# A quarter of w3 on the hardware DMA queue, q first on the software queue, and a new order of the pieces, in an attention + maxout-FFN kernel

## Chip, cores and metric

One Trainium2 chip, one of its cores. The metric is the device time of one execution in microseconds (us), as the median of several runs. PE is TensorE (matmuls and, as PEld, its weight loads), DVE is VectorE, ACT is ScalarE, POOL is GpSimd, SP is SyncE, which here only issues DMAs.

## What is computed

```
# q, k, v: (8, 8, 576, 64), phi: (8, 8, 576, 32), fp32; w1, w2, w3: (512, 768), w_out: (768, 512)
a = softmax(phi, axis=2)                       # over the sequence, per memory slot
k_m = einsum('bhsm,bhsd->bhmd', a, k)          # 32 memory rows per head
v_m = einsum('bhsm,bhsd->bhmd', a, v)
attn = softmax(q @ k_m^T / sqrt(64), axis=-1)  # over the 32 slots
x = (attn @ v_m), heads side by side           # 4608 rows of 512
h = maximum(maximum(x @ w1, x @ w2), x @ w3)
out = h @ w_out                                # (4608, 512) fp32
```

## The kernel before

The eight batches are worked on one by one, in bf16 with fp32 sums in PSUM. Four pairs of heads lie side by side, with 128 partitions each. The kernel never forms x. It multiplies v_m into the weights first (`fold`), so that the FFN's first layer runs on the attention weights. It also uses max(x w1, x w2, x w3) = max(x (w1 - w3), x (w2 - w3), 0) + x w3: the relu and the max are done on the differences, and x w3 w_out is a term of its own, for which w3 @ w_out is formed once (`w3_t` transposes w3, `w3_o` multiplies).

The program is a long list of pieces, written out by hand, each as letter, index and batch: `F3@1` is piece F3 of batch 1. The list (lines 593 to 619) is the program order on every engine. Each engine works through its own instructions in this order and waits where an input isn't there. A second list (line 138) gives the PSUM bank of each piece that uses one. The pieces:

- loads: `H` k and v of batch 0 in halves (H2, H0 are k; H3, H1 are v), `L0` phi, `L1` k, `L2` v, `L3` q, `Y0`, `Y1`, `Y2` w1, w2, w3, `Y3` w_out. All but phi of batch 0 are issued by POOL (the software queue) and cast from fp32 to bf16 on the way. phi of batch 0 goes over SP's hardware queue in fp32. Loads of POOL land in the order of their issue.
- `E` exp of phi (ACT). `r0`, `r1` pack k and v into `kvr` (`pack`, POOL). `B` multiplies a with k and v (`att_kv`, PE; from batch 2 on it reads `kvr`, and so both packs). `N` normalises (DVE). `K` transposes (PE and a copy).
- `Q` transposes q (DVE). `S` is the scores and their exp (PE, then ACT twice).
- the softmax over the slots, for each of two groups of heads: `a` transpose, `s` sum, `c` reciprocal (DVE), `m` multiply (`att_mul`, POOL), `X` transpose back (DVE). Batch 0 uses `M` and `R` (matmul with ones, logarithm and exp) in place of `a`, `s`, `c`, `m`.
- `D` folds v_m into the weights (PE and a copy). `V` forms w1 - w3 and w2 - w3 (DVE); batch 0 does without by a second term in `D`.
- `F` is the FFN's first layer: twelve pieces per batch, even ones with a relu copy, odd ones with a max on DVE. `T` is the second layer and the output's DMA. `W`, `O` are w3_t and w3_o. `Z` are matmuls on zeros (fillers) that keep PE busy while data are on their way, and `I` is the identity matrix.

`evacuate` (line 166) does the copies out of PSUM: a table `EVAC` names ACT or DVE for each piece, and a `!` behind the piece in the list swaps the two. `issue` (line 561) hands the `!` to the pieces K, D, F, T, W and O. The other kinds of piece don't take it.

```
"m": lambda: att_mul(b, i),                # no swap: POOL
"D": lambda: fold(b, i, swap),
```

Of the kernel before, what the change touches and what calls it, by code (L numbers as in the profile page):

```python
# [8 lines left out]
FP32 = mybir.dt.float32  # L9
# [6 lines left out]
def kernel(  # L16
# [12 lines left out]
    nc = tc.nc  # L29

    B, H, S, D = q.shape
    M = phi.shape[-1]
    P = 128
    NP = H // 2
    NG = NP // 2
    HP = P // 2
    NC = S // HP
    R = 32
    DM = H * D
    DF = moe_w1.shape[1]  # L40
# [5 lines left out]
    inp = ctx.enter_context(tc.tile_pool(name="inp", bufs=2))  # L46
# [23 lines left out]
    w_sb = const.tile([P, NP, 3, DF], BF16, name="w_sb")  # L70
# [7 lines left out]
    def by_pair(src, b):  # L78
        return src[b].rearrange("h s d -> (h s) d").rearrange(
            "(j p c) d -> p j (c d)", p=P, c=NC  # L80
        )
# [1 line left out]
    halves = [slice(0, NP // 2), slice(NP // 2, NP)]  # L83

    def load_ph(b):
        ph = inp.tile([P, NP, NC, M], FP32, name="ph")
        loaded.setdefault(b, {})["ph"] = ph
        dst = ph.rearrange("p j c m -> p j (c m)")
        if b == 0:
            for h in halves:  # L90
                nc.sync.dma_start(out=dst[:, h], in_=by_pair(phi, b)[:, h])
        else:
            nc.gpsimd.dma_start(out=dst, in_=by_pair(phi, b))

    def load_kv(b, i, h=slice(0, NP)):
        kv = loaded.setdefault(b, {})["kv"] = kvos[b % 2]
        nc.gpsimd.dma_start(  # L97
            out=kv[:, 1 - i, h].rearrange("p j c d -> p j (c d)"),
            in_=by_pair((k, v)[i], b)[:, h],
        )  # L100

    def pack(b, i):
        nc.gpsimd.tensor_copy(  # L103
            out=kvrs[b % 2][:, :, :, D * i : D * (i + 1)], in_=kvos[b % 2][:, 1 - i]
        )

    def load_q(b):
        qq = inp.tile([P, NP, NC, D], BF16, name="qq")
        loaded.setdefault(b, {})["q"] = qq
        nc.gpsimd.dma_start(  # L110
            out=qq.rearrange("p j c d -> p j (c d)"), in_=by_pair(q, b)
        )

    def load_w(i):
        w = (moe_w1, moe_w2, moe_w3)[i]
        nc.gpsimd.dma_start(
            out=w_sb[:, :, i], in_=w.rearrange("(j p) f -> p j f", p=P)
        )

    ident = const.tile([P, P], BF16, name="ident")  # L120
# [1 line left out]
    def load_wo():  # L122
        nc.gpsimd.dma_start(out=wo_sb, in_=moe_w_out.rearrange("(t p) c -> p t c", p=P))

    load_ph(0)

    warm = const.tile([P, BANK], BF16, name="warm")
    nc.vector.memset(warm, 0.0)  # L128
# [4 lines left out]
    for i in range(P // M):  # L133
# [4 lines left out]
    banks = iter(  # L138
        "".join(
            """  # L140
            00224460026701101401264026402640264026452063420643064206420642064562074206742064
            20642064201640264102640264026402640264072406247026402640264024602406520462046204
            62704267402640264124602416420642064206420642067676767670
            """.split()
        )
    )
# [78 lines left out]
    def att_exp(b, js=slice(0, NP)):  # L225
        s = st.setdefault(b, {})
        if "e" not in s:
            s["e"] = work.tile([P, NP, NC, M], BF16, name="e")
        nc.scalar.activation(out=s["e"][:, js], in_=loaded[b]["ph"][:, js], func=AF.Exp)  # L229
# [8 lines left out]
    def att_kv(b, part=None):  # L238
        s = st[b]
        kvp = two_banks()  # L240
        s["kvp", part] = kvp
        kv = loaded[b]["kv"]
        nd = {None: 2 * D + 1, 0: 2 * D, 1: D}[part]
        kvr = kvrs[b % 2]
        for c in range(NC):
            for j in range(NP):
                for a in range(NG):
                    r = slice(HP * a, HP * (a + 1))
                    nc.tensor.matmul(  # L249
                        kvp[M * j : M * (j + 1), a, 0:nd],  # L250
                        lhsT=s["e"][r, j, c, :],
                        rhs={
                            None: lambda: kvr[r, j, c, 0:nd],
                            0: lambda: k_and_ones(kv, r, j, c),
                            1: lambda: kv[r, 0, j, c, :],
                        }[part](),
                        start=(c == 0),
                        stop=(c == NC - 1),
                        tile_position=(HP * a, M * j),
                    )  # L260
# [141 lines left out]
    def att_rec(b, g):  # L402
        s = st[b]
        nc.vector.reciprocal(out=s["sm", g], in_=s["sm", g])  # L404
# [156 lines left out]
    def issue(b, n, swap):  # L561

        i = int(n[1:]) if len(n) > 1 else None
        {
            "I": lambda: [make_identity(nc, ident)]
            + [nc.gpsimd.memset(x[:, :, :, 2 * D : 2 * D + 1], 1.0) for x in kvrs],
            "Y": lambda: load_w(i) if i < 3 else load_wo(),
            "L": lambda: load_ph(b) if i == 0 else load_q(b) if i == 3 else load_kv(b, i - 1),
            "H": lambda: load_kv(b, i % 2, halves[i // 2]),
            "r": lambda: pack(b, i),  # L570
            "E": lambda: [att_exp(b, h) for h in (halves if b == 0 else [slice(0, NP)])],
            "B": lambda: att_kv(b, i),
            "N": lambda: att_kv_norm(b, i),
            "K": lambda: att_kv_t(b, swap, i),
            "Q": lambda: att_q(b, i),
            "S": lambda: att_score(b),
            "a": lambda: att_t(b, i),
            "s": lambda: att_sum(b, i),
            "c": lambda: att_rec(b, i),
            "m": lambda: att_mul(b, i),  # L580
            "X": lambda: (ones_mul if (b, i) in ONES else att_back)(b, i),
            "M": lambda: ones_sum(b, i),
            "R": lambda: ones_rec(b, i),
            "D": lambda: fold(b, i, swap),
            "F": lambda: ffn1(b, i, swap),
            "T": lambda: ffn2(b, i, swap),
            "W": lambda: w3_t(i, swap),
            "O": lambda: w3_o(i, swap),
            "V": lambda: w_diff(i),
            "Z": lambda: warm_up(i),  # L590
        }[n[0]]()


    for w in """
        E@0 H2@0 H0@0 L3@0 Z25@0 B0@0 Y2@0 I@0 N0@0 Z2@0 K0@0! Q0@0 Q1@0 Z9@0 S@0 Z2@0 M0@0 M1@0
        R0@0 R1@0 W0@0 Y3@0 W1@0 W2@0 Z6@0 O1@0 H3@0 O3@0 O2@0 H1@0 X1@0 B1@0 X0@0 N1@0
        K1@0 O0@0 Y0@0 D1@0! D0@0! D3@0 F8@0 F10@0 F2@0 V0@0 F6@0 F0@0! Y1@0 D2@0 D4@0 F4@0
        L0@1 V1@0 F1@0 E@1 F3@0 L1@1 F5@0 F9@0 F7@0 L3@1 F11@0 B0@1 T3@0 N0@1 K0@1! L2@1 Q1@1
        L2@2 L1@2 Q0@1 L0@2 V2@0 T0@0! L3@2 S@1 T1@0 a0@1 s0@1 c0@1 m0@1 B1@1 N1@1 a1@1 L1@3
        K1@1 s1@1 D0@1 D1@1! D2@1 c1@1 m1@1 X0@1 L3@3 r1@2 X1@1 T2@0! L2@3 F6@1 F10@1 F7@1 F2@1  # L600
        F3@1 F4@1 F0@1 r0@2 E@2 F5@1 F1@1 F11@1 L0@3 L0@4 F8@1 L2@4 F9@1 B@2 D3@1 N@2 Q1@2
        T0@1! K@2 T2@1! r0@3 Q0@2 S@2 a0@2 a1@2 s1@2 c1@2 m1@2 T4@1! D1@2! s0@2 D2@2 c0@2 m0@2
        X1@2 D0@2 T3@1 Q0@3 L3@4 X0@2 Q1@3 T1@1 F0@2 F4@2 F8@2 F6@2 F9@2 E@3 F7@2 r1@3 F5@2
        F10@2 F1@2 B@3 L1@4 D3@2 N@3 L0@5 F2@2 F11@2 E@4 F3@2 L1@5 K@3 r1@4 L2@5 T2@2! S@3 T3@2
        a0@3 s0@3 c0@3 m0@3 D0@3 D2@3 a1@3 s1@3 c1@3 X0@3 D1@3! Q0@4 m1@3 T1@2 L3@5 L2@6 T0@2!
        X1@3 F10@3 r0@4 F2@3 F4@3 E@5 Q1@4 r0@5 F5@3 F3@3 L1@6 F8@3 B@4 N@4 D3@3 F9@3 F6@3
        F11@3 L0@6 K@4 F0@3 F7@3 F1@3 S@4 a0@4 T4@3! s0@4 a1@4 D0@4 c0@4 s1@4 r1@5 c1@4 D3@4
        m0@4 X0@4 Q0@5 T0@3! D1@4! D2@4 B@5 T3@3 m1@4 X1@4 L0@7 F10@4 Q1@5 N@5 F8@4 K@5 F6@4
        F9@4 S@5 F7@4 L3@6 F2@4 F4@4 a0@5 L1@7 a1@5 F0@4 s0@5 r1@6 F3@4 D0@5 r0@6 s1@5 c1@5 E@6
        D3@5 m1@5 c0@5 F1@4 T1@3 L2@7 F11@4 L3@7 E@7 F5@4 m0@5 B@6 D1@5! D2@5 X1@5 N@6 T2@3!  # L610
        X0@5 F6@5 F8@5 Q0@6 Q1@6 K@6 F4@5 F9@5 S@6 F7@5 r0@7 a0@6 F2@5 a1@6 s0@6 c0@6 F0@5
        F10@5 m0@6 F1@5 s1@6 c1@6 F11@5 F5@5 T0@4! F3@5 X0@6 T2@4! r1@7 D0@6 D1@6! Q0@7 B@7
        m1@6 N@7 X1@6 T2@5! K@7 T3@4 Q1@7 S@7 a0@7 F2@6 s0@7 a1@7 s1@7 c1@7 m1@7 c0@7 F4@6
        T4@5! D3@6 D2@7 D0@7! T0@5! D3@7 D2@6 X1@7 m0@7 D1@7! T1@4 X0@7 F6@7 F3@6 T1@5 F4@7
        F8@7 F0@7 F5@6 F10@6 F7@7 F9@7 F10@7 F5@7 F0@6 F11@7 F6@6 F1@7 F7@6 F2@7 F8@6 F11@6
        F9@6 F1@6 F3@7 T0@6! T0@7! T3@5 T2@7! T2@6! T1@6 T1@7 T3@6 T4@7! T3@7
    """.split():
        n, b = w.rstrip("!").split("@")
        issue(int(b), n, w.endswith("!"))
# [30 lines left out]
```

## Time and profile before

| what | value |
|---|---|
| median of 3 runs | 164.98 us (164.94 to 165.61) |
| span of the profiled execution | 163.3 us |
| granted TensorE clock, mean | 0.995 |
| bytes by the software queue (POOL) | 21.43 MB, 68.7% of 16 engines' span |
| bytes by SP's hardware queue | 9.90 MB, 17.2% |
| longest group on PE | F, line 466: 384 matmuls, 50.5 us |
| longest group on POOL | packs, line 103: 12 of 2.11 us |
| multiplies on POOL, line 409 | 14 of 1.15 us |

The profile is of one execution. Its span is counted from the first to the last instruction. The times of the runs are those of whole executions, and are somewhat longer. "L103" is line 103 of the kernel. The matmuls of PE overlap, so a group's mean is longer than what one adds to the time.

### The profile page before, as it was taken

The numbers are of one execution on the slowest core, as the hardware profiler recorded it, in microseconds if no ns is written. First come the engines' busy times: TensorE is split into PE (matmuls) and PEld (weight loads), VectorE is DVE, ScalarE is ACT, GpSimd is POOL, SyncE is SP. The second block draws the span as 40 slices with busy tenths as digits, with TensorE's granted clock in tenths as the row PEclk, the third lists the DMA queues.
The fourth block names the chain that finished last, engine by engine and source line by source line (L and its number), as shares of the span: only waits on it lengthen the run. The fifth ranks groups of instructions, "written<-read, shape, count | busy, mean of one in ns | idle before, by whom it ended". The sixth has DMA issues, their size and how long they took to land.

```text
span 163.3 us, 4838 instructions
## 1 busy us (share of the span) xinstructions
PE 153.8 (94%) x2080; PEld 85.3 (52%) x2080; DVE 90.4 (55%) x181; ACT 100.6 (62%) x151; POOL 69.5 (43%) x71
## 2 busy tenths in 40 slices
PE   7978798899899999999999999999999999999990
PEld 2433444564377436743673575576553468744450
DVE  2023704798838665849399748879749128810010
ACT  4205445845497488778885899994658976223320
POOL 7932205100599259657968957646403100000000
PEclk9999999999999999999999999999999999999998
DMA  6999999999999999999999999996313130014333
GB/s 150 152 206 207 205 210 217 274 208 210 253 313 238 209 253 379 274 210 293 252 263 206 232 355 264 191 233 150 130 69 129 69 128 0 0 68 186 135 128 130
DMA packets 21974, 31.77 MB, mean 195 GB/s; under 512 B 1216, under 2 KB 16576, under 8 KB 21952
## 3 DMA queue, kind: packets, MB, share of 16 engines
q0 software_dynamic: 16080, 21.43, 68.7%
q1 hardware_dynamic: 5728, 9.90, 17.2%
q8 instruction: 16, 0.26, 0.6%
q10 hardware_dynamic: 144, 0.13, 0.2%
q14 instruction: 6, 0.05, 0.1%
HBM read 39.32 MB, written 9.44 MB: 299 GB/s over the span
## 4 chain that ended last, share of the span: by engine, by line
PE 83%; DMA 9%; POOL 2%; ACT 2%; issue 1%; DVE 1%; ACTq 0%; POOLq 0%
PE psum L497 29%; PE psum L466 28%; DMA wo_sb<-in_moe_w_out_dram 9%; PE psum L506 8%; PE psum L440 6%; PE psum L249 4%; PE psum L192 3%; PE psum L333 2%; PE psum L515 1%; ACT h L170 1%; PE psum L538 1%; PE psum L298 1%; POOL kvo L97 1%; ACT wp L172 1%; POOL qq L110 0%
## 5 line engine op out<-in xcount | busy, mean ns | idle before, releaser
L497 PE MATMUL psum<-wo_sb,hT 128*128 128x512 bf16 x210 | 51.3, 380 | 0.0
L466 PE MATMUL psum<-attn,wp 128*128 128x288 bf16 x384 | 50.5, 286 | 0.1
L479 DVE TENSOR_TENSOR hT<-psum,h 128x576 bf16<-128x576 f32 x48 | 34.2, 749 | 18.0 <-PE psum L466 12.5
L466 PEld LDWEIGHTS <-wp 128*128 128x128 bf16 x384 | 36.7, 98 | 13.2 <-issue 2.0
L172 ACT COPY ot<-psum 128x512 f32<-128x512 f32 x35 | 20.7, 591 | 32.1 <-PE psum L506 25.2
L497 PEld LDWEIGHTS <-hT 128*128 128x128 bf16 x210 | 19.2, 97 | 24.0 <-issue 4.3
L172 ACT CAST wp<-psum 128x1024 bf16<-128x1024 f32 (+1 forms) x31 | 29.2, 995 | 3.8 <-PE psum L440 2.0
L103 POOL COPY kvr<-kvo 128x2304 bf16<-128x2304 bf16 x12 | 25.3, 2111 | 13.7 <-DMA kvo<-in_k_dram 10.1
L170 ACT ACTIVATE h<-psum 128x576 bf16<-128x576 f32 x47 | 28.4, 659 | 3.5 <-PE psum L466 3.3
L409 POOL TENSOR_TENSOR t<-t,sm 128x576 bf16<-128x576 bf16 x14 | 16.1, 1154 | 24.6 <-DVE sm L404 24.4
L506 PE MATMUL psum<-wp,attn 128*128 128x512 bf16 x62 | 18.4, 379 | 0.0
L159 PE MATMUL psum<-warm 128*128 128x512 bf16 x44 | 12.1, 427 | 1.2 <-DVE warm L128 1.2
L313 DVE STREAM_TRANSPOSE qT<-qq 128x576 f32<-128x576 f32 x16 | 11.7, 747 | 1.4 <-DMA qq<-in_q_dram 1.4
L342 ACT ACTIVATE e<-psum 128x576 bf16<-128x576 f32 x16 | 9.6, 652 | 3.8 <-PE psum L333 3.8
L229 ACT ACTIVATE e<-ph 128x1152 bf16<-128x1152 f32 (+1 forms) x9 | 9.6, 1065 | 1.7 <-DMA ph<-in_phi_dram 1.6
L395 DVE TENSOR_REDUCE sm<-t 128x18 f32<-128x576 bf16 x14 | 10.3, 738 | 0.2
L387 DVE STREAM_TRANSPOSE t<-e 128x288 f32<-128x288 f32 x14 | 6.4, 465 | 6.2 <-ACT e L342 6.1
L97 POOL DMA_DIRECT2D kvo<-in_v_dram x9 | 6.7, 749 | 7.1 <-PE psum L249 4.1
L506 PEld LDWEIGHTS <-attn 128*128 128x128 bf16 x62 | 6.1, 98 | 7.1
L110 POOL DMA_DIRECT2D qq<-in_q_dram x8 | 6.2, 770 | 6.6 <-DVE h L174 3.7
L555 DVE COPY ot<-psum 128x256 f32<-128x256 f32 x1 | 0.4, 425 | 15.4 <-PE psum L546 15.4
L249 PEld LDWEIGHTS <-e 64*32 64x32 bf16 x720 | 6.9, 90 | 3.7 <-issue 3.3
(57 smaller groups left out, 114.4 us busy)
## 6 DMA issues: line engine op xcount, KB each, us to landing
out_dram<-ot SPq DMA_DIRECT2D x35, 256.0 KB, 5.6
qq<-in_q_dram POOLq DMA_DIRECT2D x8, 576.0 KB, 12.2
ph<-in_phi_dram POOLq DMA_DIRECT2D x7, 576.0 KB, 14.4
kvo<-in_k_dram POOLq DMA_DIRECT2D x7, 576.0 KB, 14.6
kvo<-in_v_dram POOLq DMA_DIRECT2D x7, 576.0 KB, 15.6
w_sb<-in_moe_w_dram POOLq DMA_DIRECT2D x3, 768.0 KB, 19.0
wo_sb<-in_moe_w_out_dram POOLq DMA_DIRECT2D x1, 768.0 KB, 14.6
ph<-in_phi_dram SPq DMA_DIRECT2D x2, 288.0 KB, 3.0
```

The costliest lines, as they stand in the source:

```text
L103: nc.gpsimd.tensor_copy(out=kvrs[b % 2][:, :, :, D * i : D * (i + 1)], in_=kvos[b % 2][:, 1 - i])
L159: nc.tensor.matmul(po[:, 0:BANK], lhsT=warm[:, 0:P], rhs=warm, start=True, stop=True)
L170: nc.scalar.activation(out=out_, in_=in_, func=AF.Relu)
L172: nc.scalar.copy(out=out_, in_=in_)
L249: nc.tensor.matmul(kvp[M * j : M * (j + 1), a, 0:nd], lhsT=s["e"][r, j, c, :], rhs={None: lambda: kvr[r, j, c, 0:nd], 0: lambda: k_and_one ...
L313: nc.vector.transpose(out=s["qT"][:, j].rearrange("p j c r e -> p (j c r e)").bitcast(FP32), in_=loaded[b]["q"][:, j].rearrange("p j c d - ...
L395: nc.vector.tensor_reduce(out=sm, in_=s["t", g].rearrange("p n r e -> p n e r"), op=ALU.add, axis=mybir.AxisListType.X,)
L409: nc.gpsimd.tensor_tensor(out=t, in0=t, in1=s["sm", g].unsqueeze(2).to_broadcast([P, S // HP, R, 2]), op=ALU.mult,)
L466: nc.tensor.matmul(acc[:, h, 0:SH], lhsT=wps[b][:, g, w * DF + ft * P : w * DF + (ft + 1) * P], rhs=attn[:, g, c0 : c0 + SH], start=(g == ...
L479: nc.vector.tensor_tensor(out=hT[:, ft, (b % 2) * S : (b % 2 + 1) * S].rearrange("p (h n) -> p h n", h=2), in0=a, in1=s["h1", ft], op=ALU.max,
L497: nc.tensor.matmul(po, lhsT=hT[:, fc, c0 : c0 + P], rhs=wo_sb[:, fc, :], start=(n == 0), stop=False,)
L506: nc.tensor.matmul(po, lhsT=attn[:, g, c0 : c0 + P], rhs=wp3s[b][:, g, :], start=False, stop=(g == NG - 1),)
```

## The change

- `load_w(2)` leaves out the first 128 rows of w3. They are loaded in fp32 by SP, behind phi of batch 0, into a tile `w3f` that takes one of the two buffers of phi, and are cast by a new piece `G` (`G0` on DVE).
- `L3@0` (q of batch 0) is the first piece, ahead of k; the identity (`I`) goes behind w_out's load.
- All pieces have a new order and new banks. The same 368 pieces are there, and `G0@0`. The `!` marks are new, too: 15 of the 48 relu copies are on DVE (1 before), and 7 of the 36 copies of `T` that go through `evacuate` (none before).

```diff
     def load_ph(b):
-        ph = inp.tile([P, NP, NC, M], FP32, name="ph")
+        ph = inp.tile([P, NP, NC, M], FP32, name="ph", tag="ph")
...
     def load_w(i):
         w = (moe_w1, moe_w2, moe_w3)[i]
+        j = slice(1 if i == 2 else 0, NP)
         nc.gpsimd.dma_start(
-            out=w_sb[:, :, i], in_=w.rearrange("(j p) f -> p j f", p=P)
+            out=w_sb[:, j, i], in_=w.rearrange("(j p) f -> p j f", p=P)[:, j]
         )
...
     load_ph(0)
+
+    w3f = inp.tile([P, NP, NC, M], FP32, name="w3f", tag="ph")
+    w3f = w3f.rearrange("p j c m -> p (j c m)")[:, 0:DF]
+    nc.sync.dma_start(out=w3f, in_=moe_w3[0:P])
+
+    def cast_w3(i):
+        if i:
+            nc.scalar.copy(out=w_sb[:, 0, 2], in_=w3f)
+        else:
+            nc.vector.tensor_copy(out=w_sb[:, 0, 2], in_=w3f)
...
+            "G": lambda: cast_w3(i),
...
     for w in """
-        E@0 H2@0 H0@0 L3@0 Z25@0 B0@0 Y2@0 I@0 N0@0 Z2@0 K0@0! Q0@0 Q1@0 Z9@0 S@0 Z2@0 M0@0 M1@0
-        R0@0 R1@0 W0@0 Y3@0 W1@0 W2@0 Z6@0 O1@0 H3@0 O3@0 O2@0 H1@0 X1@0 B1@0 X0@0 N1@0
-        K1@0 O0@0 Y0@0 D1@0! D0@0! D3@0 F8@0 F10@0 F2@0 V0@0 F6@0 F0@0! Y1@0 D2@0 D4@0 F4@0
-        L0@1 V1@0 F1@0 E@1 F3@0 L1@1 F5@0 F9@0 F7@0 L3@1 F11@0 B0@1 T3@0 N0@1 K0@1! L2@1 Q1@1
-        L2@2 L1@2 Q0@1 L0@2 V2@0 T0@0! L3@2 S@1 T1@0 a0@1 s0@1 c0@1 m0@1 B1@1 N1@1 a1@1 L1@3
-        K1@1 s1@1 D0@1 D1@1! D2@1 c1@1 m1@1 X0@1 L3@3 r1@2 X1@1 T2@0! L2@3 F6@1 F10@1 F7@1 F2@1
-        F3@1 F4@1 F0@1 r0@2 E@2 F5@1 F1@1 F11@1 L0@3 L0@4 F8@1 L2@4 F9@1 B@2 D3@1 N@2 Q1@2
-        T0@1! K@2 T2@1! r0@3 Q0@2 S@2 a0@2 a1@2 s1@2 c1@2 m1@2 T4@1! D1@2! s0@2 D2@2 c0@2 m0@2
-        X1@2 D0@2 T3@1 Q0@3 L3@4 X0@2 Q1@3 T1@1 F0@2 F4@2 F8@2 F6@2 F9@2 E@3 F7@2 r1@3 F5@2
-        F10@2 F1@2 B@3 L1@4 D3@2 N@3 L0@5 F2@2 F11@2 E@4 F3@2 L1@5 K@3 r1@4 L2@5 T2@2! S@3 T3@2
-        a0@3 s0@3 c0@3 m0@3 D0@3 D2@3 a1@3 s1@3 c1@3 X0@3 D1@3! Q0@4 m1@3 T1@2 L3@5 L2@6 T0@2!
-        X1@3 F10@3 r0@4 F2@3 F4@3 E@5 Q1@4 r0@5 F5@3 F3@3 L1@6 F8@3 B@4 N@4 D3@3 F9@3 F6@3
...
+        L3@0 Q0@0 H2@0 H0@0 Y2@0 Z25@0 Z6@0 E@0 Y3@0 G0@0 Q1@0 I@0 B0@0 Z9@0 N0@0 H3@0
+        K0@0! H1@0 Y0@0 W1@0! W0@0 S@0 Z2@0 M0@0 W2@0! Z2@0 O1@0! M1@0 R0@0 O0@0! B1@0
+        R1@0 N1@0 O2@0 X1@0 X0@0 K1@0! Y1@0 O3@0 D1@0! D0@0 F8@0! V0@0 L0@1 L1@1 D3@0
+        F2@0 F10@0 F4@0 F0@0! D2@0 D4@0 L3@1 F6@0 V1@0 L2@1 F1@0 E@1 F3@0 F7@0 F9@0 L0@2
+        F5@0 B0@1 L1@2 F11@0 N0@1 Q0@1 Q1@1 T0@0! V2@0 K0@1! T3@0 S@1 a0@1 B1@1 L2@2
+        N1@1 a1@1 E@2 s0@1 T1@0 c0@1 m0@1 K1@1 s1@1 c1@1 X0@1 m1@1! D0@1 L0@3 X1@1 D2@1
+        L3@2 L2@3 D1@1! T2@0! F6@1 F0@1! F7@1 F10@1 F11@1 F8@1 F4@1! F1@1 L3@3 F2@1 F3@1
+        F5@1 F9@1 r0@2 r1@2 B@2 N@2 Q1@2 D3@1 Q0@2 T0@1! K@2! L1@3 E@3 L1@4 T2@1 r1@3
+        S@2 a0@2 a1@2 L2@4 T4@1! s1@2 c1@2 D2@2 s0@2 L0@4 D1@2! c0@2 m1@2 m0@2! D0@2
+        T1@1 T3@1 X0@2 X1@2 F8@2 Q1@3 r0@3 L0@5 F10@2! F4@2 F9@2 F5@2 F0@2 F11@2 F1@2
+        D3@2 B@3 N@3 F2@2 F3@2 F6@2 F7@2 Q0@3 L3@4 K@3! r0@4 L2@5 T2@2! S@3 a0@3 E@4
+        a1@3 s1@3 s0@3 c0@3 m0@3! L1@5 r1@4 T3@2 c1@3 L3@5 D3@3 D1@3! L0@6 D0@3 m1@3
+        X0@3 T1@2 B@4 X1@3 L1@6 N@4 r1@5 Q1@4 T0@2! Q0@4 F4@3 F8@3 F0@3! r0@5 L2@6
+        K@4 F1@3 F10@3 L3@6 E@5 F9@3 F11@3 L2@7 F6@3 F5@3 F2@3 F7@3 S@4 a0@4 B@5 D2@4
+        F3@3 N@5 T4@3! D1@4! s0@4 D3@4 c0@4 D0@4 a1@4 s1@4 c1@4 m0@4 T3@3 K@5! X0@4 Q1@5
+        Q0@5 T0@3! m1@4 S@5 L0@7 X1@4 r0@6 F10@4! F6@4 F8@4 a1@5 a0@5 L1@7 F4@4! s0@5
...
```

More of the change, by code (lines that the diff above doesn't have):

```diff
@@ L140 @@
             """
-            00224460026701101401264026402640264026452063420643064206420642064562074206742064
-            20642064201640264102640264026402640264072406247026402640264024602406520462046204
-            62704267402640264124602416420642064206420642067676767670
+            01023204612455642542462406240620462046234260230625602460420640264524636402304206
+            24026402467426240724604602460426042604246032604260426046204620460274062042406240
+            42064201670246407042624620462060246204264654624602323230
             """.split()
@@ L607 @@
[L607 to L616, printed above, removed]
+        L3@0 Q0@0 H2@0 H0@0 Y2@0 Z25@0 Z6@0 E@0 Y3@0 G0@0 Q1@0 I@0 B0@0 Z9@0 N0@0 H3@0
+        K0@0! H1@0 Y0@0 W1@0! W0@0 S@0 Z2@0 M0@0 W2@0! Z2@0 O1@0! M1@0 R0@0 O0@0! B1@0
@@ new lines @@
+        S@2 a0@2 a1@2 L2@4 T4@1! s1@2 c1@2 D2@2 s0@2 L0@4 D1@2! c0@2 m1@2 m0@2! D0@2
+        T1@1 T3@1 X0@2 X1@2 F8@2 Q1@3 r0@3 L0@5 F10@2! F4@2 F9@2 F5@2 F0@2 F11@2 F1@2
+        D3@2 B@3 N@3 F2@2 F3@2 F6@2 F7@2 Q0@3 L3@4 K@3! r0@4 L2@5 T2@2! S@3 a0@3 E@4
+        a1@3 s1@3 s0@3 c0@3 m0@3! L1@5 r1@4 T3@2 c1@3 L3@5 D3@3 D1@3! L0@6 D0@3 m1@3
+        X0@3 T1@2 B@4 X1@3 L1@6 N@4 r1@5 D2@3 Q1@4 T0@2! Q0@4 F4@3 F8@3 F0@3! r0@5 L2@6
+        K@4 F1@3 F10@3 L3@6 E@5 F9@3 F11@3 L2@7 F6@3 F5@3 F2@3 F7@3 S@4 a0@4 B@5 D2@4
@@ new lines @@
+        F3@3 N@5 T4@3! D1@4! s0@4 D3@4 c0@4 D0@4 a1@4 s1@4 c1@4 m0@4 T3@3 K@5! X0@4 Q1@5
+        Q0@5 T0@3! m1@4 S@5 L0@7 X1@4 r0@6 F10@4! F6@4 F8@4 a1@5 a0@5 L1@7 F4@4! s0@5
+        s1@5 D3@5 D0@5 c1@5 c0@5 r1@6 F7@4 T1@3 F9@4 E@6 F0@4! m1@5 F2@4 F11@4 L3@7 F5@4
+        D2@5 X1@5 Q1@6 m0@5 D1@5! X0@5 B@6 N@6 T2@3! F8@5! F1@4 Q0@6 K@6! F3@4 F10@5
+        F4@5! F0@5 F6@5 Q0@7 F2@5 T1@4 Q1@7 S@6 F1@5 E@7 F7@5 F9@5 T0@4! F5@5 r0@7 r1@7
+        F3@5 D1@6! B@7 a0@6 s0@6 N@7 D0@6! F11@5 T3@4! K@7 T2@4! T2@5! D3@6 a1@6 c0@6
@@ L617 @@
+        D0@7 s1@6 m0@6 D2@7! c1@6 T0@5! m1@6! X1@6 S@7 X0@6 a0@7 s0@7 T4@5! a1@7 D3@7
+        c0@7 m0@7 D2@6 D1@7 T1@5 F6@6 s1@7 c1@7 X0@7 m1@7 F4@6 F10@6 X1@7 F7@6 F5@6
+        F11@6 F8@7 F8@6! F0@6! T3@5! F9@6 F2@6 F3@6 F1@6 F2@7 F9@7 F6@7 F4@7! F0@7! T3@6
+        F5@7 T2@6 T1@6 F10@7 F11@7 F3@7 F1@7 F7@7 T0@6 T1@7 T2@7 T4@7! T0@7 T3@7
     """.split():
```

## The prediction

> **What bounds the kernel now.** I read the page first, then the waits of PE, the chain of waits in order of time, the clock and DMA share in narrow windows, and last the timelines of POOL, DVE and PE around the pieces that the new order moves. The page:
>
> ```profile
> span 163.3 us, 4838 instructions
> PE 153.8 (94%) x2080; PEld 85.3 (52%) x2080; DVE 90.4 (55%) x181; ACT 100.6 (62%) x151; POOL 69.5 (43%) x71
> DMA  6999999999999999999999999996313130014333
> ```
>
> PE works 94% of the span, and the DMA engines are full for the first 27 of 40 slices. The waits of PE (us in total, times, longest):
>
> ```profile
> PE psum L192 <- DMA wo_sb<-in_moe_w_out_dram: 1.0, 1, 1.0
> PE psum L298 <- DVE kvn L273: 0.9, 2, 0.4
> PE psum L249 <- DMA kvo<-in_k_dram: 0.8, 1, 0.8
> PE psum L440 <- ACT h L170: 0.6, 1, 0.6
> PE psum L440 <- DVE kvt L176: 0.3, 1, 0.3
> ```
>
> The timeline places them. The last PE wait is the 0.32 us that ends at 43.45 (kvt). From there to 159.6 PE stands still for no more than a few hundredths. So the rest of the order gives nothing away: a wait that the new order makes there lengthens the kernel by its whole size, and a gain can only come from before 43.5. The 0.6 us that is put down to ACT ends at 30.72, when w2 lands (issued at 8.0, 22.7 us to landing): a DMA wait. The loads in flight set the first 30 us: w3 lands at 15.8, wo at 19.6, w1 at 26.2 and w2 at 30.7.
>
> **The load part.** A quarter of w3 leaves the software queue. wo, of 768 KB, landed 3.8 us after w3, so 192 KB less is worth 0.94 us to all that follows. Against it stands the SP load, 393 KB of fp32. SP's own phi ran at 366 and 373 GB/s in the windows 2.5 to 3.5, which makes 1.06 us of DMA time. Part of that is free: the DMA share is 0.66 and 0.81 in the two half microseconds from 4.0, where it is 1.2 once the software queue runs, a hole of 0.47 us. Net gain: 0.94 - (1.06 - 0.47) = 0.35 us. The ends are -0.1 (no hole used) and +0.94 (all hidden). [...]
>
> q first, k behind it: w3 stands behind all three in both orders, so only B0@0 moves, from 9.3 to about 12.6 (q lands where the second k half did, 9.05 plus up to 0.6, and k takes q's 3.05 us after it). Nine fillers and W1, W0 now stand ahead of S@0, which goes from 13.2 to about 16.7; w3T is complete at about 19.5, when wo (19.3) is there. Nothing is lost, but O1@0 gains only 0.2. The cast of w3f is one DVE copy of 128x768, between 0.5 (684 ns for 1024 bf16) and 1.2 us (1225 ns for 1024 from PSUM to bf16); DVE waits for k there, so 0. Without that cover it would delay Q1@0, which has 4 us. M1@0 (0.24 us) moves behind wo, into the wait for w2. D2@0 then starts at about 30.35 instead of 30.72.
>
> PE has the same matmuls (44 fillers in both). Fourteen more relu copies (758 ns) and seven of the output copies go from ACT to DVE; DVE rises from 90 to about 106 of 163 us. I take 0; in a run of FFN pieces a pair costs DVE 0.76 + 0.75 against 0.98 on PE, so each pair without slack costs 0.5.
>
> **The order on POOL, where the cost is.** Packs (2.11 us), multiplies (1.15) and load issues (0.74 to 0.80) share POOL, in program order. Four multiplies carry the mark `!` in the new list (m1@1, m0@2, m0@3, m1@6), but att_mul doesn't read it: all fourteen stay on POOL. What is queued behind them counts. The pieces of batch 3 and 4 before:
>
> ```profile
> 72.19 0.49 PE L333 MATMUL psum<-qT,kvt 32*32 32x288 bf16 x32
> ...
> 81.71 0.80 PE L249 MATMUL psum<-kvr,e 64*32 64x129 bf16 x72
> ```
> ```profile
> 71.38 2.11 POOL L103 COPY kvr<-kvo 128x2304 bf16<-128x2304 bf16 x1 [2.30 <-DMA kvo<-in_v_dram]
> 73.43 0.74 POOL L97 DMA_DIRECT2D kvo<-in_v_dram  x1
> 75.11 1.15 POOL L409 TENSOR_TENSOR t<-t,sm 128x576 bf16<-128x576 bf16 x1 [0.95 <-DVE sm L404]
> 76.54 1.15 POOL L409 TENSOR_TENSOR t<-t,sm 128x576 bf16<-128x576 bf16 x1 [0.27 <-DVE sm L404]
> ...
> 79.17 2.12 POOL L103 COPY kvr<-kvo 128x2304 bf16<-128x2304 bf16 x1
> ```
> ```profile
> 73.46 0.48 DVE L387 STREAM_TRANSPOSE t<-e 128x288 f32<-128x288 f32 x1 [1.82 <-ACT e L342]
> 73.98 0.75 DVE L395 TENSOR_REDUCE sm<-t 128x18 f32<-128x576 bf16 x1
> 74.76 0.27 DVE L404 RECIPROCAL sm<-sm 128x18 f32<-128x18 f32 x1
> 74.94 0.42 DVE L387 STREAM_TRANSPOSE t<-e 128x288 f32<-128x288 f32 x1
> ```
>
> S@3 is at 72.19, m0@3 at 75.11, r0@4 ends at 81.29 and B@4, which reads it, runs at 81.71: 0.42 us of slack. r1@4 (71.38) was done before S@3.
>
> **B@4.** The new order puts m0@3, L1@5, r1@4 on POOL after S@3, and a1 and s1 on DVE before c0. m0@3 starts 2.92 + 0.42 + 0.75 = 4.09 after S@3; its 1.15, the issue's 0.74 and the pack's 2.11 make 8.1. PE has S (0.42), T3 (1.83), three D (0.77) and T1 (1.73) for it: 4.75. B@4 waits 3.4 us, and all of PE behind it. Its v has landed long before. Ends: 2.6 (PE is late itself) to 4.0 (a queue ahead of c0).
>
> **B@2.** m0@1 began 2.93 after S@1 (39.49); N1 (0.29) and a1 (0.47) are put ahead of c0: 3.69. Then on POOL m0 1.16, a gap of 0.1, m1 1.15, four load issues (3.1; L0@3, L3@2, L2@3, L3@3) where there were three, and both packs (4.22) at the end: 13.4 us. Between D2@0 and S@1 lie the same pieces as before; S@1 goes 0.35 earlier with D2@0 and loses some 0.2 to B0@1, which now comes one FFN piece earlier than k@1 (34.8 before). So S@1 at 39.3, B@2 at 52.7 instead of 51.94: **+0.8**. All is done by then that was done by B@2 before, and nothing of the gains ahead is left: they, and the two waits of 0.75 us that T1@0 now covers, end in this wait. ACT points the same way, as E@2 stands ahead of T1's copy and waits for phi, which lands after v@1 (40.5). Ends: -0.4, +1.4.
>
> **Smaller ones.** r1@3 stands ahead of L2@4, L0@4, m1@2, m0@2 and waits for v@3, which lands third after v@2 (about 57.4); packed at 59.5, POOL is free at 61.0, where m1@2 could start at 60.7: F8@2 loses 0.3 to 1.3, I take **0.5**. Behind r1@4, m1@3 has two more issues ahead of it: 0.8 + 0.75 + 1.15 + X1 0.47 = 3.2 after B@4's start, PE has 0.73 + 0.25 + 1.73 = 2.7: **0.4** for F4@3. Batch 4's X1 stands behind N@5 and both Q@5 on DVE: **0.3**. The last pieces end as before.
>
> Sum: 0.8 + 0.5 + 3.4 + 0.4 + 0.3 = 5.4. The profiled span goes from 163.3 to 168.7. The median of the runs, 164.98, is 1.7 above the span; I keep that: **170.4**.
>
> **Rivals.**
> 1. The clock drops in the long wait. In the windows of the tail PE ends at 159.6 and the granted clock falls to 0.50 by 161.75, 2.1 us later; no wait before that is longer than 1.2 us, so the trace has no drop inside the work. At the start the fillers take 427 ns each until 4.6 and 213 ns after, 3.4 us at half speed. A drop in the wait of 3.4 us costs half of such a 3.4 us: +1.7, 172.1. Against it: one idle stretch, and the tail shows one delay only. [...]
> 2. Only the queue at B@4 bites: the loads are worth 0.9 and B@2 finds its packs done. 3.4 - 0.9 = +2.5, 167.5. For it: the queue there needs no estimate of a landing.
> 3. The other side, faster: the chain to r1@4 is short enough. This needs the pack to end within 4.75 us of S@3, where the rows give 8.1. Then the gain of the loads (0.35) and the two covered waits (0.75) reach the end: -1.1, 163.9. For it: PE has no other reason to be late. Against it: POOL's program order.
> 4. No change to tell: the waits add up to no more than the 1.1 that is gained. The SP load doing nothing (software loads no earlier) belongs here or adds 0.35 to the others.
>
> **Chances.** The forecast 0.52, clock 0.20, only B@4 0.17, faster 0.06, no change 0.05. A measurement of this kernel tells about 0.5% (0.8 us) from nothing. The first three are slower by more, 0.89; of rival 3 0.05 is beyond the bound, so faster 0.05 and the same 0.06. The range runs from rival 2 less 0.4, 167.1, to rival 1 plus 0.9 for a few DVE pairs and the upper ends, 173.0.
>
> **What would show it.** In the timeline of POOL: two packs back to back right before B@2 and four issues ahead of them; m0@3, a load issue and a pack in one row before B@4, with PE idle some 3.4 us and the pack (L103) named as its releaser. In the waits of PE: POOL kvr, which isn't there now, at some 4 us in total. wo landing at 19.2 to 19.3, and w2 at about 30.3. In the windows after B@4: the granted clock at 1.00, or 0.5 for rival 1. I'm wrong if PE never waits for kvr, or if B@4 starts less than 6 us after S@3.

## The result and the profile after

The changed kernel takes 172.66 us in the median of four runs (171.86 to 173.44), the kernel before 165.03 (four runs, 164.94 to 165.61). The ratio is 1.0448, with a 95% interval of 1.0411 to 1.0486. It is slower by 7.6 us. 5.4 were forecast as the likeliest, and 7.1 with the drop of the clock.

The page of the profile after, in the lines that were shown of before, and the granted clock by slices:

```profile
span 171.1 us, 4841 instructions
PE 156.9 (92%) x2080; PEld 86.8 (51%) x2080; DVE 104.3 (61%) x199; ACT 90.8 (53%) x134; POOL 69.5 (41%) x71
PEclk9995799999999999999879999999999999999999
DMA  5999999999989999999999999990113230113243
```

PE is busy 3 us longer with the same 2080 matmuls. The clock row says why: it falls twice, in slices 4 and 5 (about 12.8 to 21 us) and slices 20 and 21 (about 81 to 90 us). The waits of PE in the profile after (us in total, times, longest):

```profile
PE psum L260 <- DMA kvo<-in_k_dram: 4.3, 1, 4.3
PE psum L260 <- POOL kvr L103: 4.1, 2, 3.3
PE psum L170 <- DVE warm L139: 1.2, 1, 1.2
```

The first wait has grown: it is B@0 for k (line 260 is att_kv), and it was 0.8 us before. The second is new. It is for the packs, twice: B@2 (0.79) and B@4 (3.29). The third, at the very start, is as long as before. PE's timeline places the first two (start, length, with the wait before it in brackets):

```profile
14.52 1.16 PE L260 MATMUL psum<-kvo,e 64*32 64x128 bf16 x72 [4.31 <-DMA kvo<-in_k_dram]
15.62 3.89 PE L170 MATMUL psum<-warm 128*128 128x512 bf16 x9
...
22.84 1.46 PE L203 MATMUL psum<-wo_sb,w3T 128*128 128x512 bf16 x6
...
33.44 0.30 PE L451 MATMUL psum<-w_sb,kvt 64*32 64x256 bf16 x8
...
55.18 0.80 PE L260 MATMUL psum<-kvr,e 64*32 64x129 bf16 x72 [0.79 <-POOL kvr L103]
...
75.82 0.48 PE L344 MATMUL psum<-qT,kvt 32*32 32x288 bf16 x32
...
84.03 1.17 PE L260 MATMUL psum<-kvr,e 64*32 64x129 bf16 x72 [3.29 <-POOL kvr L103]
```

These are B@0, the nine fillers behind it, O1@0, D2@0, B@2, S@3 and B@4. The nine fillers take 3.9 us; in the profile before nine of them took 2.1. B@0 and B@4 themselves take 1.16 and 1.17 us, where a B takes 0.80 at full clock.

POOL in the profile after, ahead of B@4 (L2@5, m0@3, L1@5, r1@4):

```profile
74.07 0.74 POOL L97 DMA_DIRECT2D kvo<-in_v_dram  x1
79.95 1.15 POOL L420 TENSOR_TENSOR t<-t,sm 128x576 bf16<-128x576 bf16 x1 [5.14 <-DVE sm L415]
81.06 0.80 POOL L97 DMA_DIRECT2D kvo<-in_k_dram  x1
81.86 2.12 POOL L103 COPY kvr<-kvo 128x2304 bf16<-128x2304 bf16 x1
```

The pack's v has landed before; it only waits for its turn behind the multiply. It ends at 83.98, and B@4 starts at 84.03.

The last matmul ends 8.34 us later than before (167.92 against 159.58). Taken from the pieces' starts: D2@0 is 2.72 later (33.44 against 30.72). From D2@0 to B@2 the new order takes 0.52 more, and from B@2 to S@3 0.39 more. S@3 to B@4 has the wait of 3.29. The 1.42 that is left lies behind B@4, where the clock is low at first.

### The profile page after: what moved, and what is told of

It reads as the page before. It is cut to its first block, busy times and chain, and to the rows that moved or that the text cites. A ratio compares the mean times of both kernels' runs of the same rounds, so it can differ in the third digit from the quotient of the medians.

```text
span 171.1 us, 4841 instructions
## 1 busy us (share of the span) xinstructions
PE 156.9 (92%) x2080; PEld 86.8 (51%) x2080; DVE 104.3 (61%) x199; ACT 90.8 (53%) x134; POOL 69.5 (41%) x71
## 4 chain that ended last, share of the span: by engine, by line
PE 66%; DMA 13%; POOL 10%; issue 4%; ACT 3%; DVE 1%; POOLq 0%; ACTq 0%
PE psum L477 23%; PE psum L508 20%; DMA kvo<-in_k_dram 7%; DMA kvo<-in_v_dram 6%; PE psum L517 6%; PE psum L260 4%; POOL kvr L103 4%; PE psum L451 4%; POOL t L420 3%; PE psum L203 3%; PE psum L170 2%; POOL kvo L97 2%; POOL qq L110 1%; PE psum L526 1%; PE psum L344 1%
## 5 line engine op out<-in xcount | busy, mean ns | idle before, releaser
L508 PE MATMUL psum<-wo_sb,hT 128*128 128x512 bf16 x210 | 52.2, 385 | 0.1
L183 ACT COPY ot<-psum 128x512 f32<-128x512 f32 x28 | 16.6, 593 | 34.5 <-PE psum L517 23.5
L183 ACT CAST wp<-psum 128x1024 bf16<-128x1024 f32 (+1 forms) x30 | 28.3, 998 | 8.5 <-PE psum L451 7.8
L181 ACT ACTIVATE h<-psum 128x576 bf16<-128x576 f32 x33 | 20.7, 656 | 10.7 <-PE psum L477 10.6
L324 DVE STREAM_TRANSPOSE qT<-qq 128x576 f32<-128x576 f32 x16 | 11.6, 751 | 10.2 <-DMA qq<-in_q_dram 10.2
L185 DVE TENSOR_SCALAR h<-psum 128x576 bf16<-128x576 f32 x15 | 11.1, 749 | 7.7 <-PE psum L477 6.7
L170 PE MATMUL psum<-warm 128*128 128x512 bf16 x44 | 14.1, 487 | 1.2 <-DVE warm L139 1.2
L260 PEld LDWEIGHTS <-e 64*32 64x32 bf16 x720 | 7.5, 97 | 11.1 <-issue 10.1
L428 DVE STREAM_TRANSPOSE attn<-t 128x288 f32<-128x288 f32 x14 | 6.2, 457 | 11.3 <-POOL t L420 11.2
L183 ACT COPY kvt<-psum 128x384 bf16<-128x384 bf16 (+2 forms) x7 | 3.0, 429 | 15.0 <-PE psum L309 15.0
L187 DVE COPY ot<-psum 128x512 f32<-128x512 f32 x7 | 4.8, 690 | 8.7 <-PE psum L517 8.1
## 6 DMA issues: line engine op xcount, KB each, us to landing
qq<-in_q_dram POOLq DMA_DIRECT2D x8, 576.0 KB, 10.7
kvo<-in_k_dram POOLq DMA_DIRECT2D x7, 576.0 KB, 12.9
```

Of the source, the lines that this page charges most:

```text
L170: nc.tensor.matmul(po[:, 0:BANK], lhsT=warm[:, 0:P], rhs=warm, start=True, stop=True)
L181: nc.scalar.activation(out=out_, in_=in_, func=AF.Relu)
L183: nc.scalar.copy(out=out_, in_=in_)
L185: nc.vector.tensor_scalar_max(out=out_, in0=in_, scalar1=0.0)
L260: nc.tensor.matmul(kvp[M * j : M * (j + 1), a, 0:nd], lhsT=s["e"][r, j, c, :], rhs={None: lambda: kvr[r, j, c, 0:nd], 0: lambda: k_and_one ...
L324: nc.vector.transpose(out=s["qT"][:, j].rearrange("p j c r e -> p (j c r e)").bitcast(FP32), in_=loaded[b]["q"][:, j].rearrange("p j c d - ...
```

## The experiments

All are compared by the place of a few pieces in the profile (D2@0, B@2, B@4, B@5) as well as by the median, since the runs of one kernel scatter by up to 2.3 us.

**The loads: which part makes them late.** In the profile after, q lands at 11.6 us, and the second half of k at 14.4, where I had 9.05 to 9.6 and 12.6. Two theories: A, the SP load takes DMA time from q. B, a whole q at the head of the software queue starts slowly.

The first run has all of w3 in the software load again:

```diff
-        j = slice(1 if i == 2 else 0, NP)
+        j = slice(0, NP)
...
-    nc.sync.dma_start(out=w3f, in_=moe_w3[0:P])
...
-        ... Z6@0 E@0 Y3@0 G0@0 Q1@0 ...
+        ... Z6@0 E@0 Y3@0 Q1@0 ...
```

> The changed kernel, with all of w3 on the software queue again and the SP load of w3 and its cast left out. Measured for the changed kernel: q lands at 11.5, the SP load of w3 at 11.1, the second k half at 14.4, w3 at 17.1, w_out at 21.1 us; PE idles 10.2 to 14.5, the granted clock is 0.5 from about 12.5 to 19.4, D2@0 starts at 33.4; median 172.66. Theory A (the SP load is what makes the first loads late: its packets share the DMA engines with q from 4 to 11 us): q lands at about 9.6, the second k half at 12.5, w3 at 16.2, w_out at 20.0; the idle before B@0 shrinks from 4.3 to about 2.4 us; D2@0 at about 31.5, median about 170.8. Rival B (a load of q as one whole piece at the head is what is slow): q lands at 11 or later still, k at 14 or later, w3 0.9 later than now, median 172.7 to 173.6.

The second moves the k halves ahead of q and keeps the SP load:

```diff
-        L3@0 Q0@0 H2@0 H0@0 Y2@0 ...
+        H2@0 H0@0 L3@0 Q0@0 Y2@0 ...
```

> The changed kernel, with the two k halves ahead of q in the software queue as before the change, and the SP load of w3 kept. Theory A: k's second half lands where q does now, at 11.2 to 11.6 us, q at 14.4, w3 and w_out stay at 17.1 and 21.1; B@0 starts at about 11.6 and the clock doesn't drop; w_out then sets O1@0 at about 21.4 instead of 22.8: median about 171.2. Rival B: k lands at 9 to 9.5 as before the change, q at 12.2, w3 at 15, w_out at 18.7 to 19.3; D2@0 at 30.4 to 30.9, median about 170.

The third has both edits, and the fourth is the kernel before with the SP load and its cast alone (`Q1@0 G0@0 Z9@0 S@0`):

> Both undone: the changed kernel with the loads of before (no SP load of w3, k halves ahead of q), only the order of the pieces behind them new. Both theories: k's second half lands at about 9.1, q at 12.1, w3 at 15.8, w_out at 19.6; the clock stays at 1.00 until the wait at B@4; D2@0 starts at 30.5 to 31.2. What is left against before is then the new order: waits at B@2 (about 0.8), B@4 (3.3) and the clock's drop behind it (about 1.2); median 169.5 to 170.5.

> The kernel before with only the SP load of a quarter of w3 (and its cast on DVE behind Q1@0) added; order, banks and the place of q as before. The prediction's step: wo lands 0.35 us earlier (19.2 to 19.3), median 164.6 to 165.0. Theory A: k's second half lands at 11.2 instead of 9.05, w_out at about 21 instead of 19.6, D2@0 1 to 1.5 us later; median 166 to 166.6. Rival B: no loss, as the prediction had it.

In the fifth, q is at the head as in the first, without the SP load, but in two halves:

```diff
-        nc.gpsimd.dma_start(
-            out=qq.rearrange("p j c d -> p j (c d)"), in_=by_pair(q, b)
-        )
+        for h in halves if b == 0 else [slice(0, NP)]:
+            nc.gpsimd.dma_start(
+                out=qq.rearrange("p j c d -> p j (c d)")[:, h], in_=by_pair(q, b)[:, h]
+            )
```

> The changed kernel without the SP load (as in the run that loads w3 in one piece by software), and q of batch 0 at the head in two halves instead of one piece. With q in one piece there q landed at 10.4, the second k half at 13.2, w3 at 17.0, w_out at 20.95; with k's two halves at the head: 9.05, q 11.9, w3 15.9, w_out 19.7. If it is the one large piece at the head that starts the software queue slowly: q's second half lands at 9 to 9.3, k at 11.9 to 12.2, w3 at 15.9 to 16.1, w_out at 19.7 to 20. If it is what is loaded (q and its place): q at 10 or later, w_out at 20.7 or later. In time at most 1.2 us, and the clock's drops can hide it: median 171.3 to 172.8.

Landings in us (issue plus time to landing, by the trace's list of DMA issues), and the start of D2@0:

| kernel | first 576 KB | second 576 KB | w3 | w_out | D2@0 | median |
|---|---|---|---|---|---|---|
| before | 9.1 (k) | 12.1 | 15.8 | 19.6 | 30.72 | 165.03 |
| after (q whole, SP load) | 11.6 (q) | 14.4 | 17.2 | 21.1 | 33.44 | 172.66 |
| q whole, no SP load | 10.5 (q) | 13.3 | 17.0 | 20.9 | 31.67 | 172.83 |
| k halves first, SP load | 10.9 (k) | 13.7 | 17.2 | 20.6 | 32.18 | 172.00 |
| k halves first, no SP load | 9.1 (k) | 11.9 | 15.9 | 19.8 | 32.13 | 172.59 |
| kernel before + SP load | 10.7 (k) | 13.5 | 16.3 | 20.2 | 30.84 | 165.61 |
| q in two halves, no SP load | 8.9 (q) | 12.0 | 15.7 | 19.6 | 30.38 | 172.41 |

Both theories hold, each for a part. The SP load makes the first 576 KB land 1.1 to 1.8 us later, whatever they are. It doesn't pay this back: in the kernel before, w_out lands 0.6 later for it, and not 0.35 earlier. Each row is one profile, and profiles with the same first loads scatter. Over all kernels of this document, a whole q with the SP load lands at 10.9 to 11.6 (five profiles) and w_out behind it at 20.4 to 22.1; k in halves without the SP load lands at 8.4 to 9.1 (five) and w_out at 19.3 to 19.9. So differences of a few tenths tell nothing here. The SP load issues at 1.74 and lands 9.4 us later in the profile after, where phi's halves ahead of it took 3 us each:

```profile
qq<-in_q_dram POOLq DMA_DIRECT2D x1, 576.0 KB, 10.3
w3f<-in_moe_w_dram SPq DMA_DIRECT2D x1, 384.0 KB, 9.4
```

(The list of DMA issues of the profile after: queue, count, size, us to landing.) The SP load's packets stood among those of the software queue from 4 to 11 us (16.7% of the 16 engines' time against 63.1% from 4 to 5 us, 20.6 against 78.9 from 7 to 8). The hole that I had it fill was hardly smaller for it: the DMA shares of the two half microseconds from 4.0 are 0.94 and 0.65, against 0.66 and 0.81 before. A whole q at the head costs 1.6 us at its own landing and 1.3 at w_out's (20.9 against 19.6), against the same bytes in two halves. Why one piece of 576 KB starts the queue more slowly than two halves was not found out. The two costs don't add up at w_out: with q whole, it is 0.2 later with the SP load than without, which is within the scatter.

The loads moved by this, and the medians hardly. For q whole without the SP load, k halves first with it, and k halves first without it, 170.8, 171.2 and 169.5 to 170.5 were expected; 172.83, 172.00 and 172.59 came.

With k halves first and no SP load, loads are as before, and D2@0 is still 1.4 us late. There N0@0 waits behind Q0 and Q1 on DVE, for q. PE stands for 1.66 us until N0@0 is done, and soon after for 1.50 until w3 has landed; the clock is at half from 14.8 to 21.7 us. With q in two halves and on time, the new first pieces start D2@0 at 30.38. The prediction had 30.35, but the agreement is partly luck: it counted on 0.35 from the SP load, which this run doesn't have, and the four profiles with the first pieces of before have D2@0 anywhere from 29.91 to 31.07.

```profile
12.10 0.80 PE L252 MATMUL psum<-kvo,e 64*32 64x128 bf16 x72 [2.12 <-DMA kvo<-in_k_dram]
...
19.60 1.46 PE L195 MATMUL psum<-wo_sb,w3T 128*128 128x512 bf16 x6 [0.28 <-DMA wo_sb<-in_moe_w_out_dram]
```

(PE's timeline of the run with q in two halves: B@0 and O1@0.) O1@0 begins when w_out lands. In the profile after, w_out was there 1.8 us before O1@0, so there the loads alone didn't set it.

**The clock.** Fillers are put into the idle stretches, with nothing else changed: 14 ahead of B@4 (into a PSUM bank that is free there), and in another run 21 more ahead of B@0 (`Z27@0` in place of `Z6@0`).

```diff
-        X0@3 T1@2 B@4 X1@3 ...
+        X0@3 T1@2 Z14@4 B@4 X1@3 ...
```

> The changed kernel with 14 fillers (matmuls on zeros, 3.0 us at full clock) put ahead of B@4, in its 3.3 us wait; nothing else changes. If the drop of the clock after B@4 is caused by the idle stretch: B@4 starts at the same place, the granted clock stays at 1.00 from 80 us on and 1.2 to 1.4 us are saved; median 171.3. If the drop has another cause, the clock still falls and the median stays at 172.7.

> The changed kernel with 21 more fillers ahead of B@0 (27 in place of 6), which cover the idle stretch from 10.2 to 14.5 us. If the slow clock there is what makes O1@0 start 1.7 us after w_out has landed: clock 1.00 up to 80 us, B@0 at 14.5 as now, O1@0 at 20.9 to 21.4 instead of 22.8, D2@0 at 31.6 to 32; median 171.0. If the loads and the order set it alone: O1@0 within 0.4 of 22.8, median 172.4 to 172.8.

The granted clock in windows of 2 us (columns: window, length, busy time and count of PE, PEld, DVE, ACT, POOL, then the clock, DMA share, GB/s). First the profile after, then the run with fillers ahead of B@4:

```profile
14.00:16.00 2.00, 1.48 (x73) 1.05 (x74) 0.22 (x2) 0.00 (x0) 1.03 (x2) 0.50 1.19 204
...
84.00:86.00 2.00, 1.97 (x82) 1.18 (x82) 0.00 (x0) 0.32 (x1) 1.99 (x3) 0.52 1.20 213
86.00:88.00 2.00, 2.00 (x7) 0.75 (x6) 1.34 (x6) 0.69 (x1) 2.00 (x3) 0.62 1.17 266
```
```profile
84.00:86.00 2.00, 2.00 (x26) 0.83 (x10) 0.14 (x1) 1.01 (x1) 1.99 (x3) 1.00 1.17 236
86.00:88.00 2.00, 1.99 (x18) 1.50 (x17) 1.97 (x7) 1.70 (x3) 2.00 (x2) 1.00 1.19 234
```

With fillers the clock stays up, PE runs 26 matmuls in 84 to 86 us, and the median is 171.21: 1.45 us less, with B@4 still 8.21 us behind S@3. So the drop comes from the idle stretch. Its price is less plain. F1@3 starts 5.85 us behind B@4 in the profile after and 4.51 with the fillers, 1.34 sooner. But two pieces on, at F9@3, PE then waits 0.35 for DVE, whose queue behind X1@3 is late. From B@4 to the last matmul 0.83 us are saved (83.06 against 83.89), so 0.6 of the 1.42 stays with the clock up. The rest of what this profile gains lies ahead of B@4, which starts 0.76 earlier (83.27): at the start the clock was low for 3.5 us in this execution, and not for 6.9. That 1.45 and 1.42 are so close is luck.

Fillers ahead of B@0 keep the clock up there, too (1.00 in every 0.1 us from 8 to 24): O1@0 is at 21.12 and D2@0 at 31.71, 1.73 earlier than in the changed kernel and where "q whole, no SP load" has it. In time nothing came of it: the median is 173.96. B@4 starts 1.7 earlier, but behind it the clock is low for 6.9 us and not 3.6. Besides, PE stands still for 1.16 us up to 99.1 in that profile, with no releaser shown. What that is stayed open. The clock doesn't explain the median: all four runs of this kernel (173.58 to 174.12) are above the changed kernel's, also the one with a granted clock of 0.998 (173.58).

**The wait at B@4.** One pack is moved ahead of the multiply:

```diff
-        ... K@3! r0@4 L2@5 T2@2! S@3 a0@3 E@4 a1@3 s1@3 s0@3 c0@3 m0@3! L1@5 r1@4 T3@2
+        ... K@3! r0@4 L2@5 r1@4 T2@2! S@3 a0@3 E@4 a1@3 s1@3 s0@3 c0@3 m0@3! L1@5 T3@2
```

> The changed kernel with one pack moved: r1@4 stands behind L2@5, ahead of m0@3 and L1@5 on POOL; all else as in the changed kernel. Theory (POOL's order at batch 3 is what makes B@4 wait 3.3 us, and the clock's drop comes from this wait): no PE wait for kvr at B@4, the granted clock stays 1.00 after 80 us; 3.3 + 1.3 = 4.6 us less, median 168.0. Rival (v or another input is as late as the pack): B@4 still waits over 1 us, median 170 or more.

Median 170.72, 1.9 less. The wait at B@4 is gone, and the clock stays at 1.00 behind it: POOL's order was its cause. But most of it comes back in the next pieces. PE's waits in this run:

```profile
PE psum L260 <- POOL kvr L103: 2.1, 2, 1.3
PE psum L477 <- DVE rden L280: 1.3, 1, 1.3
...
PE psum L477 <- DVE h L185: 0.3, 1, 0.3
```

B@2 waits 0.8 as before. F4@3 now waits 1.3 for X1@3, which still has its multiply behind two load issues, F9@3 waits 0.3 for a relu copy that stands behind X1@3 on DVE, and B@5 waits 1.3 for its pack. I had expected 168.0.

The other edit reads the `!` of the four marked multiplies and puts them on DVE:

```diff
-    def att_mul(b, g):
+    def att_mul(b, g, swap):
...
-        nc.gpsimd.tensor_tensor(
+        (nc.vector if swap else nc.gpsimd).tensor_tensor(
...
-            "m": lambda: att_mul(b, i),
+            "m": lambda: att_mul(b, i, swap),
```

> The changed kernel, with the `!` of m1@1, m0@2, m0@3 and m1@6 read: these four multiplies run on DVE, the other ten on POOL. If the list was made for multiplies that can move: the packs before B@2 and B@4 end 1.2 us and 2 to 4 us earlier, both PE waits for kvr (0.8 and 3.3) go and with them the clock's drop; median 167.0 to 167.6. Rival: DVE pays 0.75 us for each and is late for X and the max of F instead: new PE waits on DVE of 1 us or more, median 168.5 or more.

Both waits for packs, at B@2 and B@4, are gone, which agrees with a list made for multiplies that can move. But the median is 172.20. A wait of 3.63 us stands at B@5 in their place, for k's pack, with 6.9 us of low clock. Neither expectation had that.

**The order without its late start.** The pieces and loads of before up to F4@0, and the new order behind it (banks 2, 3 and 4, 5 exchanged); then the same with the four multiplies on DVE; then with k of batch 5 moved up in the software queue:

```diff
-        ... L0@5 ... L3@4 ... L2@5 ... L1@5
+        ... L0@5 L1@5 ... L3@4 ... L2@5
```

> The pieces of the kernel before, with its loads, up to F4@0 behind D4@0; from there on the changed kernel's order (banks 2, 3 and 4, 5 exchanged there, F4@0 in place of F6@0, L0@1 and L1@1 as the first loads behind). Theory: the new order of the first 30 us with its loads costs 2.7 us, the rest about 5: D2@0 starts at 30.7 as before, the clock is 1.00 up to 80 us, B@2 at 52.3 to 52.9 with a wait for kvr of 0.8, B@4 at 81.0 to 81.6 with a wait of 3.3, then the clock's drop (1.2 to 3); median 169.5 to 171. Rival (the late start is hidden later by POOL and the loads anyway): B@4 at 83 or later, median 172 or more.

> The same with the four marked multiplies on DVE. In the changed kernel this took the waits at B@2 and B@4 away, and a wait of 3.6 us for k's pack at B@5 and seven us of half clock came in their place. Theory (the loads of k@5 are late because of their place in the software queue, whatever PE does): B@5 starts at 90 to 91 again and waits 4 us or more, as PE is there 1.5 us earlier; median 170.5 to 172. Rival (the wait at B@5 came from the late start): B@5 waits less than 2 us, no drop of the clock, median 166 to 168.

> As the run before, with one load moved: k of batch 5 (L1@5) stands right behind phi of batch 5 in the software queue, ahead of q@4 and v@5. Theory: k@5 lands some 6 us earlier, B@5 waits less than 1 us for its packs, unless q@4 or v@5, now one load later each, come late themselves (S@4 then waits 1 to 2 us); the clock doesn't drop; median 166 to 168. Rival: DMA as a whole is behind at this place, so that another load is as late: a wait of 3 us or more at S@4 or B@5, median 170 or more.

The first gives 170.49 (ratio 1.0354, interval 1.0304 to 1.0405): B@4 at 81.74 with its 3.29, a drop of the clock of 3.5 us. So the new order behind the start costs some 5.4 us by itself, and the start some 2. One of the four runs had a granted clock of 1.00 and took 170.11, so most of the 5.4 isn't clock.

With the multiplies on DVE it is 170.61. B@5 waits 3.02 us for the pack of k. The packs of batch 5 in this run, and in the kernel before:

```profile
83.94 2.11 POOL L103 COPY kvr<-kvo 128x2304 bf16<-128x2304 bf16 x1 [3.87 <-PE psum L464]
87.58 2.11 POOL L103 COPY kvr<-kvo 128x2304 bf16<-128x2304 bf16 x1 [1.54 <-DMA kvo<-in_k_dram]
```
```profile
83.07 2.11 POOL L103 COPY kvr<-kvo 128x2304 bf16<-128x2304 bf16 x1 [1.78 <-DMA kvo<-in_k_dram]
...
87.36 2.11 POOL L103 COPY kvr<-kvo 128x2304 bf16<-128x2304 bf16 x1 [0.74 <-DMA kvo<-in_v_dram]
```

Both kernels have the last of the two loads at 87.4 to 87.6. The loads aren't behind. PE is ahead: it is at B@5 at 86.7, while the order before has other pieces for it until 91.3.

With k@5 moved up, the median is 172.20. PE waits 2.80 us for DVE, which stands for q@4, and 2.55 at B@5 for the packs, as v@5 is now the late one. The rival that I had written down holds: another load is as late.

## Why the prediction came out as it did

- **POOL's order at B@4** was right in mechanism and size. S@3 to B@4 takes 8.21 us, where 8.1 were worked out, and the wait is 3.29 against 3.4. Moving the one pack takes it away.
- **B@2**: S@1 to B@2 takes 12.9 us (13.4 forecast), and B@2 waits 0.79 for the packs. It starts 3.2 later than before, though, and not 0.8, since S@1 itself was late.
- **The load part is the step that failed.** It was put at 0.35 us gained by D2@0, and D2@0 lost 2.72. The SP load was priced as 1.06 us of DMA time that partly fills a hole. It held the first software load back by 1.1 to 1.8 us instead. q first was priced at nothing, by taking q to land where k's two halves had; in one piece it came 1.6 us later, and what is behind it 1.3 (31.67 against 30.38 for D2@0, one profile each). The prediction moved B@0 from 9.3 to 12.6 and saw no loss in that; it priced the clock for the wait at B@4, but not for the idle stretch that opens here. The stretch of 4.3 us brought 6.9 us at half clock, worth the other 1.73 (33.44 against 31.71, with the fillers). In two more profiles with the same first pieces and loads the clock was low for half as long, and D2@0 came at 32.69 and 33.02. Theory A alone would have had the median fall by 1.9 without the SP load, and it didn't; B alone would have left the landings as they were.
- The rates of phi alone, 366 to 373 GB/s, were no measure for a load that runs beside another queue: the SP load of 384 KB landed 9.4 us after its issue.
- **Rival 1, the clock,** came true on top of the likeliest case. By the run with fillers the drop behind B@4 delays the next pieces by 1.3 us, of which 0.8 reach the end; 1.7 were forecast. I gave it 0.20.
- **The smaller ones**: F8@2 waits 0.22 (0.5 forecast). The 0.4 at F4@3 and the 0.3 at batch 4 don't show in the changed kernel. At half clock PE came later to F4@3. At full clock X1@3 is late, as forecast: with the fillers F9@3 loses 0.35 to the queue behind it, and with the early pack F4@3 waits 1.3.
- The copies on DVE cost nothing that shows: but for the 1.2 us at the very start, which the kernel before has too, no PE wait of more than 0.3 us is put down to DVE in the profile after.

So the sum of 5.4 is 8.3 by the trace: 3.1 more at the start, 1.4 more behind B@4 (clock for the most part), and 1.6 less behind D2@0 in the waits and the smaller ones. That the time lies so near to the 172.1 of rival 1 is therefore partly luck: the loss at the start wasn't in any of the sums, and half of it is hidden by terms that came out too large.

## What to carry to other kernels

An order of pieces has to be checked on each queue as it runs, not as its author meant it: count, for each wait that matters, everything that stands ahead of the awaited instruction on its queue. Where loads run at the DMA engines' pace for two thirds of the time, as here (8 or 9 tenths in 26 of the 40 slices of the DMA row), an order that reaches the next batch sooner gains little; in these runs, taking one wait away moved most of it to the next pack or load. An idle stretch of PE must be priced with the clock's drop behind it: in these runs 3.41 or 6.83 us at half clock. A few fillers in it are a cheap test of how much of a loss is clock, if the places of the pieces are compared and not the medians alone.

## What was not expected of the hardware

**The clock's drops came in two lengths.** In windows of 0.1 us, the 17 drops in the thirteen new profiles are 3.5 to 3.6 us (10 times) or 6.9 us long (7 times), and nothing between. By the times of the clock's changes in the traces they are 3.41 and 6.83; a window that a drop only touches counts whole.

**The length of an idle stretch didn't decide alone.** The 3.48 us ahead of B@0 gave no drop (q whole, no SP load), and 2.72 us gave one of 3.41 (kernel before + SP load). The same wait of 3.3 us ahead of B@4 gave 3.41 us at half clock in the changed kernel and 6.83 in three others (k halves first with the SP load, fillers ahead of B@0, q in two halves). What else counts stays open.

**A wait of 2.55 us was enough** for a drop of 3.41 us (B@5 in the last run), and two of 1.66 and 1.50 us with 0.3 us of work between them for one of 6.83 (k halves first, no SP load).

**The drops are not the main cause of the scatter.** The four runs without the SP load and with q whole have granted clocks of 1.00, 0.967, 0.99 and 0.99 and take 173.45, 173.24, 172.42 and 171.51: the one without a drop is the slowest. Why 1.7 to 3 us saved at the start don't show in the medians of three of these kernels (q whole without the SP load, q in two halves, fillers ahead of B@0) stays open.
